# Low words of retention's weight tiles in halves a pair apart, its first weight load a pair later, and an order for the first chain on ScalarE

## The chip, the cores and the metric

The kernel runs on one core of a Trainium2 chip. The metric is the device time of one execution in microseconds (us), taken as the median of several runs.

## The reference

Retention over 4 batches, 8 heads, 576 positions and 64 channels, then two feed-forward layers over the 2304 tokens. The first layer's activation is a quotient of two polynomials, the second's a squared ReLU.

```python
def _attn_ref(q, k, v):                     # (4, 8, 576, 64) each
    scores = scale * np.matmul(q, k.transpose(0, 1, 3, 2))
    gamma = 1.0 - 2.0 ** (-5.0 - np.arange(H, dtype=np.float32))
    Dmat = np.where(rel >= 0, gamma[:, None, None] ** rel[None, :, :], 0.0)
    return np.matmul(scores * Dmat[None, :, :, :], v)

def _moe_ref(x, w_in, w_out, a, b):         # x (2304, 512), w_in (512, 2048), w_out (2048, 512)
    h = x @ w_in
    h2 = h * h
    P = a[0] + a[1] * h + a[2] * h2 + a[3] * h2 * h
    Q = 1.0 + np.abs(b[0]) * np.abs(h) + np.abs(b[1]) * h2
    return (P / (Q + 1e-06)) @ w_out

def _moe2_ref(x, w_in, w_out, s, b):
    r = np.maximum(x @ w_in, 0.0)
    return (s * (r * r) + b) @ w_out

def reference(...):
    attn_out = _attn_ref(q, k, v)
    x = attn_out.transpose(0, 2, 1, 3).reshape(B * S, H * D)
    return _moe2_ref(_moe_ref(x, ...), ...)
```

## The kernel before

Engines: PE multiplies matrices, DVE, ACT (ScalarE) and POOL (GpSimd) work on tiles, SP issues loads. Every float operand of the layers is split into a high part (fp32r) and a low part, so each product takes three matmuls (`three`: high by low, low by high, high by high). The high part is a copy on ACT, the low part a subtraction on POOL.

**Retention** runs over 16 pairs of heads (`pairs`), one pair p per pass of the loop in `retention`. In a pass PE does, in this order: the value matmuls on the state (`value_state`, L336), the state matmuls of pair p+1 (`state`, L324), the value matmuls on the masked scores (`value_chunk`, L344), the scores of pair p+2 (`scores`, L298). The state matmuls of a pair need its values scaled by POOL (`scale`, L269), which is issued two pairs ahead. DVE masks the scores (L312) and multiplies the output with the decay (L347); ACT and POOL then split that output into `xh` (L349) and `xl` (L350), the input of the first layer. SP loads a pair four pairs ahead (`loads`), and weight tiles in between (`next_load`).

In the same loop the first three weight tiles (`W_FIRST`) are cut from their 64-bit form, as a generator of five steps a tile (`w_cut_in_halves`), of which each pass takes one or two: ACT's scaling and DVE's L178, then DVE's L181 on either half, then L185 on either half. After the last step `w_split` makes the parts of tiles 0 and 1: one high copy on ACT (L155) and two low halves on POOL (L158), the first for the tile's input weights, the second for its output weights. Tile 2 is split behind unit 0's activation in the code. Everything in the loop is issued in the order of the code (`tc.keep_in_program_order`, `pin`), but for L158, which is not pinned.

**The first layer** (`ffn`) runs over units: a unit is 512 tokens and one weight tile (or 256 tokens and two). `emit_in` issues its 12 input matmuls into one of four PSUM banks (`H_TAGS`), `rational` the activation, `out1` the 12 output matmuls (all of these matmuls have the line L475 of `three`). Units 0 to 3 have no output matmuls among them; unit 4 takes the bank of unit 0 again, once L532 has read it. `rational` of a unit is a chain: ta = |h| (L521, ACT), tq (L522, ACT), product tq*ta (L523, POOL), tt (L524, ACT), two steps on DVE (L525, L526), Ln (L527, ACT), Exp (L529, ACT), then DVE's L530, L531 and L532, the high copy gh (L534, ACT) and the low part gl (L535, POOL). The order of the layer's instructions on each engine is dealt out by a scheduler; `tc.issue_after` (here `behind`) makes an instruction come after another.

**The second layer** follows with its own loop over weight tiles; the change does not touch it.

## Time and profile before

| | us |
|---|---|
| median of 3 runs | 846.34 |
| lowest to highest | 845.95 to 848.43 |
| profiled execution | 847.38 |
| its span, first to last instruction | 845.6 |
| PE busy in the span | 832.8 |
| DVE, ACT, POOL busy | 612.5, 601.2, 392.7 |

The profile is of one execution. A row of a timeline gives the start, how long the instruction or the run of like instructions lasted, engine, line of the kernel, operation, the tiles written and read, their shape, the count, and in brackets the idle time of the engine just before with what ended it. The pair loop lies between 5 us and 75 us.

### The profile page before, as it was taken

To read this page: it belongs to the slowest core of one execution; us is meant where nothing else is said; L and a number is where in the kernel's file an instruction comes from. 1 tells how busy PE (TensorE), PEld (TensorE's weight loads), DVE (VectorE), ACT (ScalarE), POOL (GpSimd) and SP (SyncE) were. 2 spreads that over 40 slices of the span, in tenths; PEclk is the share of its full clock that TensorE was granted. 3 is DMA by queue.
4 is the path that set the end of the run, shared out by engine and by line. 5 is a ranking of instruction groups with operands and counts; after the bars stand their busy time and mean duration, and the time that the engine had idled before them with its cause. 6 is when DMAs were issued, how large, how long until landed. Compare 5 with 4: busy or idle time off the path is not lost.

```text
span 845.6 us, 13068 instructions
## 1 busy us (share of the span) xinstructions
PE 832.8 (98%) x4970; PEld 703.4 (83%) x4970; DVE 612.5 (72%) x855; ACT 601.2 (71%) x992; POOL 392.7 (46%) x324
## 2 busy tenths in 40 slices
PE   8998999999999999999999999999999999999998
PEld 7787888888888888888888888888888888888887
DVE  4776787888798878789977967788778453444445
ACT  4446998886787878689979886786667766444443
POOL 3686675465566755648856423444235221111100
PEclk9999999999999999999999999999999999999999
DMA  9983110111102101101111377555689984444302
GB/s 345 361 286 148 51 51 1 50 51 50 50 2 100 45 6 50 44 8 50 51 50 26 75 249 243 171 178 172 233 301 368 231 245 150 149 150 150 125 0 100
DMA packets 36878, 109.17 MB, mean 129 GB/s; under 512 B 3792, under 2 KB 4560, under 8 KB 31824
## 3 DMA queue, kind: packets, MB, share of 16 engines
q1 hardware_dynamic: 25952, 80.02, 26.9%
q0 software_dynamic: 10864, 28.31, 11.8%
q8 instruction: 39, 0.64, 0.3%
q14 instruction: 23, 0.19, 0.1%
HBM read 75.30 MB, written 28.84 MB: 123 GB/s over the span
## 4 chain that ended last, share of the span: by engine, by line
PE 94%; DVE 1%; POOL 1%; issue 1%; DMA 1%; ACT 1%; SPq 0%; ACTq 0%; POOLq 0%; DVEq 0%
PE o L475 23%; PE p L475 23%; PE h L475 23%; PE hB L475 7%; PE hA L475 5%; PE hG L475 5%; PE ht L475 3%; PE hs L475 3%; PE pv L344 1%; PE sc L298 1%; DMA vk<-in_qkv_dram 1%; PE pv L324 1%; PE pv L336 1%; DVE pm L312 1%; POOL w L158 0%
## 5 line engine op out<-in xcount | busy, mean ns | idle before, releaser
L475 PE MATMUL h<-xh,w 128*128 128x512 f32 (+1 forms) x640 | 184.5, 368 | 0.0
L475 PE MATMUL o<-gh,w 128*128 128x512 f32 (+1 forms) x584 | 165.8, 369 | 0.0
L523 POOL TENSOR_TENSOR tq<-tq,ta 128x512 f32<-128x512 f32 x72 | 97.5, 1354 | 89.3 <-ACT tq L522 86.0
L765 DVE TENSOR_TENSOR acc<-acc,p 128x512 f32<-128x512 f32 (+1 forms) x127 | 86.2, 680 | 72.1 <-PE p L475 71.2
L475 PEld LDWEIGHTS h<-xh,w 128*128 128x128 f32 x640 | 116.2, 188 | 20.3
L475 PE MATMUL p<-w,gh 128*128 128x512 f32 (+1 forms) x338 | 124.3, 388 | 0.0
L475 PEld LDWEIGHTS o<-gh,w 128*128 128x128 f32 x584 | 106.0, 188 | 18.4
L475 PE MATMUL h<-xl,w 128*128 128x512 f32 (+1 forms) x320 | 118.0, 369 | 0.6 <-DVE tt L532 0.6
L535 POOL TENSOR_TENSOR gl<-tt,gh 128x512 fp32r<-128x512 f32 x66 | 93.3, 1415 | 40.7 <-ACT gh L534 32.7
L475 PE MATMUL o<-gl,w 128*128 128x512 f32 (+1 forms) x292 | 107.8, 369 | 0.0
L475 PE MATMUL p<-w,gx 128*128 128x512 f32 (+1 forms) x363 | 99.3, 387 | 0.0
L163 POOL TENSOR_TENSOR w<-raw,w 128x512 fp32r<-128x512 f32 x32 | 47.4, 1511 | 78.3 <-ACT w L162 26.4
L475 PEld LDWEIGHTS p<-w,gx 128*128 128x128 f32 x363 | 67.9, 188 | 13.9
L530 DVE SCALAR_TENSOR_TENSOR tt<-tt,aneg,h 128x512 f32<-128x512 f32 x72 | 53.6, 744 | 35.3 <-ACT h L529 35.1
L475 PEld LDWEIGHTS p<-w,gh 128*128 128x128 f32 x338 | 63.4, 188 | 13.1
L527 ACT ACTIVATE ta<-tq,lnb 128x512 f32<-128x512 f32 x72 | 52.4, 729 | 24.3 <-POOL tq L523 23.5
L475 PEld LDWEIGHTS h<-xl,w 128*128 128x128 f32 x320 | 60.3, 188 | 11.2 <-DVE tt L532 1.0
L475 PE MATMUL p<-w,gl 128*128 128x512 f32 (+1 forms) x169 | 65.5, 388 | 0.0
L525 DVE TENSOR_TENSOR tt<-tt,h 128x512 f32<-128x512 f32 x72 | 49.1, 682 | 21.0 <-ACT tt L524 20.8
L475 PEld LDWEIGHTS o<-gl,w 128*128 128x128 f32 x292 | 55.1, 189 | 9.6 <-POOL gl L535 0.4
L729 ACT ACTIVATE ta<-hG 128x512 f32<-128x512 f32 x14 | 8.4, 599 | 75.9 <-PE hG L475 75.9
L521 ACT ACTIVATE ta<-h 128x512 f32<-128x512 f32 x72 | 43.2, 600 | 23.8 <-PE h L475 21.6
(150 smaller groups left out, 1816.0 us busy)
## 6 DMA issues: line engine op xcount, KB each, us to landing
raw<-in_w_dram SPq DMA_DIRECT2D x32, 1024.0 KB, 6.1
ws<-w SPq DMA_DIRECT2D x32, 512.0 KB, 8.4
w<-ws POOLq DMA_DIRECT2D x32, 512.0 KB, 5.7
xT<-in_qkv_dram SPq DMA_DIRECT2D x16, 576.0 KB, 6.3
vk<-in_qkv_dram SPq DMA_DIRECT2D x16, 480.0 KB, 6.1
sf<-ss POOLq DMA_DIRECT2D x7, 1024.0 KB, 5.1
out_dram<-acc SPq DMA_DIRECT2D x17, 256.0 KB, 3.0
acc<-acc POOLq DMA_DIRECT2D x8, 512.0 KB, 4.7
```

Of the source, the lines that this page charges most:

```text
L163: nc.gpsimd.tensor_tensor(out=dst[:, 1], in0=src, in1=f32(dst[:, 0]), op=ALU.subtract)
L298: pe(nc.tensor.matmul(sc[rows[g], j, out:out + q1 - q0], lhsT=xt[rows[j], 0, k0:k0 + Q], rhs=xt[rows[j], 1, q0:q1], start=True, stop=True, ...
L312: dve(nc.vector.tensor_tensor(out=t[:, :, 0:S], in0=sc[:, :, M0:M0 + S], op=ALU.mult, in1=mask.unsqueeze(1).to_broadcast([P, 2, S])))
L324: pe(nc.tensor.matmul(ps[r, s0:s0 + n * D].rearrange("p (n e) -> p n e", n=n), lhsT=k[:, c, j, :], rhs=v[:, c, j, :].unsqueeze(1).to_broad ...
L475: yield nc.tensor.matmul(ps, lhsT=lh, rhs=rh, start=start and x == 0, stop=stop and x == 2, skip_group_check=True)
L521: nc.scalar.activation(ta, h, AF.Abs)
L523: nc.gpsimd.tensor_tensor(out=tq, in0=tq, in1=ta, op=ALU.mult)
L525: nc.vector.tensor_tensor(out=tt, in0=tt, in1=h, op=ALU.mult)
L527: nc.scalar.activation(ta, tq, AF.Ln, bias=lnb, scale=QS)
L530: nc.vector.scalar_tensor_tensor(out=tt, in0=tt, scalar=aneg[:, 0:1], in1=r, op0=ALU.add, op1=ALU.mult)
L535: nc.gpsimd.tensor_tensor(out=gl, in0=tt, in1=f32(gh), op=ALU.subtract)]
L765: nc.vector.tensor_tensor(out=at, in0=at, in1=ps, op=ALU.add)
```

## The change

It has three parts.

1. The low halves of tiles 0 and 1 (L158) are pinned to the code's order, and the second one is put off (`owed`) to the first step of the next tile, which comes a pair later.
2. Weight tile 0 is loaded in the pass of pair 1 rather than ahead of the loop, and the cut's steps begin in the pass of pair 4 rather than 3. So tile 0 is split in pair 8 (was 7), tile 1 in pair 13 (was 12), and tile 2's five steps stand in pairs 14 (two) and 15 (three), where they stood in 13 (one), 14 and 15 (two each).
3. In `rational` unit 0's and unit 1's tt (L524) come behind their tq (L522) on ACT, and unit 1's tq behind unit 0's Ln.

```diff
--- before.py
+++ after.py
@@ -145,7 +145,10 @@
         nc.vector.scalar_tensor_tensor(out=hi, in0=hi, scalar=0x80000000, in1=t,
                                        op0=ALU.bitwise_and, op1=ALU.bitwise_or)
 
+    owed = []
+
    def w_split(kf, pinned=False):
+
         rest = tc.keep_in_program_order if pinned else free
         f = w_words(kf)[1].bitcast(F32)
         w_views(kf)
@@ -153,9 +156,16 @@
         if kf < NF:
             t, n = w_halves[i]
             rest(nc.scalar.copy(t[:, 0, n:n + 2, :], f.rearrange("p (w x) -> p w x", w=2)))
-            for x in range(2):
+
+            def low(x):
                 dst = t[:, :, n + x, :]
-                nc.gpsimd.tensor_tensor(out=dst[:, 1], in0=f[:, DM * x:DM * (x + 1)], in1=f32(dst[:, 0]), op=ALU.subtract)
+                rest(nc.gpsimd.tensor_tensor(out=dst[:, 1], in0=f[:, DM * x:DM * (x + 1)], in1=f32(dst[:, 0]), op=ALU.subtract))
+
+            low(0)
+            if pinned:
+                owed.append(lambda: low(1))
+            else:
+                low(1)
             return
         for x, y in enumerate((i, j)):
             src, dst = f[:, DM * x:DM * (x + 1)], w_half(y)
@@ -174,6 +184,8 @@
         m = wtmp.tile([P, 2 * DM], F32, tag="wm", name=f"wm{kf}")
         t = m.bitcast(U32)
         halves = [slice(DM * x, DM * (x + 1)) for x in range(2)]
+        while owed:
+            owed.pop(0)()
         pin(nc.scalar.activation(m, hi.bitcast(F32), AF.Copy, scale=2.0 ** -112))
         pin(nc.vector.tensor_scalar(lo, lo, 2.0 ** -29, 7.0, op0=ALU.mult, op1=ALU.min))
         yield
@@ -373,7 +385,6 @@
         load_decay(1, NP)
         for p in range(2, IN_BUFS):
             loads(p)
-        next_load(nc.sync, pin)
 
         steps = (s for kf in range(W_FIRST) for s in w_cut_in_halves(kf))
 
@@ -393,7 +404,7 @@
         for p in range(NPAIR):
             if p:
                 loads(p - 1 + IN_BUFS)
-            if p in (4, 8, 14, 15):
+            if p in (1, 4, 8, 14, 15):
                 next_load(nc.sync, pin)
             if p == 12:
                 small_loads()
@@ -406,7 +417,7 @@
                 scale_tail(p + 1)
             if 0 < p < NP:
                 decay(p)
-            for _ in range((p > 2) + (p > 13)):
+            for _ in range((p > 3) + (p > 13) + (p > 14)):
                 next(steps, None)
             value_chunk(p)
             if p == 14:
@@ -515,16 +526,20 @@
                 hold.enter_context(tc.issue_after(x.ins))
             return hold
 
+        first_ln = []
+
         def rational(u):
             h = hps[u]
             ta, tq, tt = [tmp_tile(u, x) for x in ("ta", "tq", "tt")]
             nc.scalar.activation(ta, h, AF.Abs)
-            nc.scalar.activation(tq, ta, AF.Identity, bias=babs[:, 0:1], scale=babs[:, 1:2])
+            with behind(*first_ln):
+                x = nc.scalar.activation(tq, ta, AF.Identity, bias=babs[:, 0:1], scale=babs[:, 1:2])
             nc.gpsimd.tensor_tensor(out=tq, in0=tq, in1=ta, op=ALU.mult)
-            nc.scalar.activation(tt, h, AF.Identity, bias=aneg[:, 2:3], scale=aneg[:, 3:4])
+            with behind(*[x][u > 1:]):
+                nc.scalar.activation(tt, h, AF.Identity, bias=aneg[:, 2:3], scale=aneg[:, 3:4])
             nc.vector.tensor_tensor(out=tt, in0=tt, in1=h, op=ALU.mult)
             nc.vector.scalar_tensor_tensor(out=tt, in0=tt, scalar=aneg[:, 1:2], in1=h, op0=ALU.add, op1=ALU.mult)
-            nc.scalar.activation(ta, tq, AF.Ln, bias=lnb, scale=QS)
+            first_ln[:] = [nc.scalar.activation(ta, tq, AF.Ln, bias=lnb, scale=QS)][u:]
             r = hps.pop(u)
             nc.scalar.activation(r, ta, AF.Exp, bias=expb, scale=-1.0)
             nc.vector.scalar_tensor_tensor(out=tt, in0=tt, scalar=aneg[:, 0:1], in1=r, op0=ALU.add, op1=ALU.mult)
```

On POOL, around pairs 12 to 15 and the first products of the layer (vk is a scaling, xl a pair's low words, w a low half, tq the product of unit 0), before:

```order
L269 TENSOR_TENSOR vk_848<-vk_848,mv 128x512
L158 TENSOR_TENSOR w_81<-raw_442,w_81 128x512 x2
L350 TENSOR_TENSOR xl<-x_942,xh 128x576
L269 TENSOR_TENSOR vk_905<-vk_905,mv 128x512
L350 TENSOR_TENSOR xl<-x_997,xh 128x576
L350 TENSOR_TENSOR xl<-x_1052,xh 128x576
L158 TENSOR_TENSOR w_81<-raw_675,w_81 128x512 x2
L523 TENSOR_TENSOR tq_1128<-tq_1128,ta_1127 128x512
```

and in the changed kernel:

```order
L281 TENSOR_TENSOR vk_847<-vk_847,mv 128x512
L362 TENSOR_TENSOR xl<-x_938,xh 128x576
L281 TENSOR_TENSOR vk_904<-vk_904,mv 128x512
L162 TENSOR_TENSOR w_81<-raw_439,w_81 128x512
L362 TENSOR_TENSOR xl<-x_993,xh 128x576
L162 TENSOR_TENSOR w_81<-raw_439,w_81 128x512
L362 TENSOR_TENSOR xl<-x_1051,xh 128x576
L162 TENSOR_TENSOR w_81<-raw_671,w_81 128x512 x2
L537 TENSOR_TENSOR tq_1128<-tq_1128,ta_1127 128x512
```

The scaling of the last pair now precedes tile 1's halves, which stand on either side of pair 13's low words; tile 2's two halves stay right in front of unit 0's product.

On DVE, from pair 14's scores to pair 15's output (raw and wm are weight tiles on their way, spre a state, x a pair's output), before:

```order
L329 TENSOR_TENSOR spre_110<-pv_974,spre_110 128x64
L178 TENSOR_SCALAR raw_675<-raw_675 128x1024
L347 TENSOR_TENSOR x_997<-pv_918,odec 128x576
L312 TENSOR_TENSOR pm_1019<-sc,mask 128x2x576
L329 TENSOR_TENSOR spre_111<-pv_1030,spre_111 128x64
L181 SCALAR_TENSOR_TENSOR wm_984<-wm_984,raw_675 128x512 x2
L347 TENSOR_TENSOR x_1052<-pv_974,odec 128x576
L414 TENSOR_SCALAR aneg<-a_sb 128x4
L185 SCALAR_TENSOR_TENSOR raw_675<-raw_675,wm_984 128x512 x2
L347 TENSOR_TENSOR x_1078<-pv_1030,odec 128x576
```

and in the changed kernel, where L341 is the former L329, L190 the former L178, L193 L181, L197 L185, L359 L347, L324 L312:

```order
L341 TENSOR_TENSOR spre_110<-pv_970,spre_110 128x64
L197 SCALAR_TENSOR_TENSOR raw_439<-raw_439,wm_749 128x512
L359 TENSOR_TENSOR x_993<-pv_917,odec 128x576
L324 TENSOR_TENSOR pm_1015<-sc,mask 128x2x576
L341 TENSOR_TENSOR spre_111<-pv_1026,spre_111 128x64
L190 TENSOR_SCALAR raw_671<-raw_671 128x1024
L193 SCALAR_TENSOR_TENSOR wm_1036<-wm_1036,raw_671 128x512
L359 TENSOR_TENSOR x_1051<-pv_970,odec 128x576
L425 TENSOR_SCALAR aneg<-a_sb 128x4
L193 SCALAR_TENSOR_TENSOR wm_1036<-wm_1036,raw_671 128x512
L197 SCALAR_TENSOR_TENSOR raw_671<-raw_671,wm_1036 128x512 x2
L359 TENSOR_TENSOR x_1078<-pv_1026,odec 128x576
```

Tile 2's first step has moved from ahead of pair 13's output to behind the state of pair 15 (the last spre), and its second L181 to behind pair 14's output; the last step of tile 1 now stands ahead of pair 13's output.

On ACT, at the first units (ta, tq, tt of unit 0 have the numbers 1127 to 1129, those of unit 1 1166 to 1168, h_1114 is unit 0's bank), before:

```order
L155 CAST w_81<-raw_675 128x1024
L521 ACTIVATE ta_1127<-h_1114 128x512
L524 ACTIVATE tt_1129<-h_1114,aneg 128x512
L522 ACTIVATE tq_1128<-ta_1127,babs 128x512
L349 CAST xh<-x_1078 128x576
L521 ACTIVATE ta_1166<-h_1150 128x512
L524 ACTIVATE tt_1168<-h_1150,aneg 128x512
L522 ACTIVATE tq_1167<-ta_1166,babs 128x512
L527 ACTIVATE ta_1127<-tq_1128,lnb 128x512
L529 ACTIVATE h_1114<-ta_1127,expb 128x512
L521 ACTIVATE ta_1198<-h_1184 128x512
L524 ACTIVATE tt_1200<-h_1184,aneg 128x512
```

and in the changed kernel, where L158 is the former L155, L534 L521, L536 L522, L539 L524, L542 L527, L544 L529:

```order
L158 CAST w_81<-raw_671 128x1024
L534 ACTIVATE ta_1127<-h_1114 128x512
L536 ACTIVATE tq_1128<-ta_1127,babs 128x512
L539 ACTIVATE tt_1129<-h_1114,aneg 128x512
L361 CAST xh<-x_1078 128x576
L534 ACTIVATE ta_1166<-h_1150 128x512
L542 ACTIVATE ta_1127<-tq_1128,lnb 128x512
L536 ACTIVATE tq_1167<-ta_1166,babs 128x512
L539 ACTIVATE tt_1168<-h_1150,aneg 128x512
L544 ACTIVATE h_1114<-ta_1127,expb 128x512
L534 ACTIVATE ta_1198<-h_1184 128x512
L539 ACTIVATE tt_1200<-h_1184,aneg 128x512
```

Unit 0's tq stands ahead of its tt; unit 0's Ln stands ahead of unit 1's tq and tt, and its Exp behind them. On DVE unit 1's second step (L526) has moved from ahead of unit 0's L530 to between unit 0's L531 and L532.

## Rows read from the trace of the kernel before

**Rows 1.** The page's first part, engines over the whole span.
```profile
PE 832.8 (98%) x4970; PEld 703.4 (83%) x4970; DVE 612.5 (72%) x855; ACT 601.2 (71%) x992; POOL 392.7 (46%) x324
```

**Rows 2.** Table by stage: stretch, length, busy time of each engine, TensorE clock, DMA.
```profile
84.00:420.00 336.00, 336.00 (x1638) 284.46 (x1639) 282.66 (x400) 275.97 (x426) 212.54 (x155) 1.00 0.12 41
```

**Rows 3.** Timeline, engine PE: start, length, line, tiles, count, idle before and releaser.
```profile
23.03 0.21 PE L298 MATMUL sc<-xT 64*64 64x64 f32 x1 [0.88 <-issue]
...
41.48 0.79 PE L298 MATMUL sc<-xT 64*64 64x64 f32 x22 [0.88 <-issue]
...
48.00 0.67 PE L324 MATMUL pv<-vk 128*64 128x128 f32 x12 [1.45 <-POOL vk L269]
48.50 1.33 PE L344 MATMUL pv<-pm,vk 128*64 128x128 f32 x20
...
67.96 0.67 PE L324 MATMUL pv<-vk 128*64 128x128 f32 x12 [2.05 <-POOL vk L269]
...
73.78 1.31 PE L344 MATMUL pv<-pm,vk 128*64 128x128 f32 x20
...
83.88 0.50 PE L475 MATMUL h<-xl,w 128*128 128x512 f32 x1 [0.58 <-DVE tt L532]
```

**Rows 4.** Timeline, engine POOL, 52 us to 79 us.
```profile
52.85 1.05 POOL L269 TENSOR_TENSOR vk<-vk,mv 128x512 f32<-128x512 f32 x1
...
62.52 2.57 POOL L158 TENSOR_TENSOR w<-raw,w 128x512 fp32r<-128x512 f32 x2 [0.34 <-ACT w L155]
65.05 1.85 POOL L350 TENSOR_TENSOR xl<-x,xh 128x576 fp32r<-128x576 f32 x1
66.87 1.04 POOL L269 TENSOR_TENSOR vk<-vk,mv 128x512 f32<-128x512 f32 x1
67.88 1.40 POOL L350 TENSOR_TENSOR xl<-x,xh 128x576 fp32r<-128x576 f32 x1
...
73.65 2.56 POOL L158 TENSOR_TENSOR w<-raw,w 128x512 fp32r<-128x512 f32 x2
77.33 1.30 POOL L523 TENSOR_TENSOR tq<-tq,ta 128x512 f32<-128x512 f32 x1 [1.11 <-ACT tq L522]
```

**Rows 5.** DMA queue q8 in 39.1:39.3, then in 46.0:46.1: packets, MB, share.
```profile
q8 instruction: 1, 0.02, 30.5%
...
q8 instruction: 1, 0.02, 63.4%
```

**Rows 6.** Timeline, engine ACT, 72 us to 81 us.
```profile
72.43 1.13 ACT L155 CAST w<-raw 128x1024 fp32r<-128x1024 f32 x1 [0.49 <-DVE raw L185]
...
77.89 0.60 ACT L521 ACTIVATE ta<-h 128x512 f32<-128x512 f32 x1
78.39 0.78 ACT L524 ACTIVATE tt<-h,aneg 128x512 f32<-128x512 f32 x1
79.05 0.81 ACT L522 ACTIVATE tq<-ta,babs 128x512 f32<-128x512 f32 x1
79.76 0.71 ACT L527 ACTIVATE ta<-tq,lnb 128x512 f32<-128x512 f32 x1
80.50 0.69 ACT L529 ACTIVATE h<-ta,expb 128x512 f32<-128x512 f32 x1
```

**Rows 7.** Timeline, engine DVE, 44 us to 84 us.
```profile
44.67 1.00 DVE L178 TENSOR_SCALAR raw<-raw 128x1024 uint32<-128x1024 uint32 x1
...
52.98 1.47 DVE L181 SCALAR_TENSOR_TENSOR wm<-wm,raw 128x512 uint32<-128x512 uint32 x1
...
63.90 1.75 DVE L178 TENSOR_SCALAR raw<-raw 128x1024 uint32<-128x1024 uint32 x1
...
69.17 1.28 DVE L181 SCALAR_TENSOR_TENSOR wm<-wm,raw 128x512 uint32<-128x512 uint32 x2
...
71.11 1.29 DVE L185 SCALAR_TENSOR_TENSOR raw<-raw,wm 128x512 uint32<-128x512 uint32 x2
...
83.14 0.68 DVE L532 SCALAR_TENSOR_TENSOR tt<-h,tt 128x512 f32<-128x512 f32 x1
```

## The prediction

> **What bounds the kernel now.** I read the page first: TensorE, PE in the rows, is busy 98% of the span [rows 1]. The table by stage comes next: from 84 us to 420 us PE is busy all of the time, at full clock [rows 2]. So time can be won or lost only where PE stands still, and that is in the pair loop and in the first units of the first layer, before 84 us. The timeline of PE shows those places [rows 3]. Two long waits are for POOL's scaling of a pair's values (L269): 1.45 us in front of pair 10's state matmuls at 48.00, and 2.05 us in front of pair 15's at 67.96. One wait of 0.58 us at 83.88 is unit 4's first matmul, which needs the PSUM bank of unit 0 and so the last step of unit 0's chain (L532, DVE). Two gaps of 0.88 us have no releaser ("issue") and lie inside a run of score matmuls, at 23.03 and 41.48.
>
> The rows of POOL say why it is late [rows 4]. At 62.52 it makes both low halves of weight tile 1 (2.57 us), then the low words of a pair (65.05), and only at 66.87 the scaling that PE waits for. The same happened at pair 10 with tile 0.
>
> **Second wait: low halves of tile 1.** Every step of a tile's cut comes one pair later, and the two halves are a pair apart. The scaling of pair 15, the last there is, now stands ahead of both halves on POOL. The wait of 2.05 goes: pair 15's state matmuls start at 65.91 instead of 67.96. What is late next there: POOL's low words of pair 12 begin 2.57 us earlier than 65.05, near 62.5, take 1.40 to 1.85, and the scaling 1.04 [rows 4]: over at 64.9 to 65.4, before PE asks at 65.91. I take the gain as 2.05, with a lower bound of 1.5 if DVE holds POOL up twice more.
>
> **First wait: low halves of tile 0.** POOL's delay of pair 10 goes in the same way, but another wait lies right behind. From the gap at 23.03 (one matmul of 36 left) to the one at 41.48 there are 253 matmuls by the loop's counts; from there to the value matmuls at 48.50 there are 126, half as many. So a block of PE's instructions ends at each, and the transfers of queue q8 (kind "instruction") agree: one packet starts between 39.1 and 39.3, and PE goes on at 41.48, some 2.3 us later; the next starts between 46.0 and 46.1 [rows 5], so PE can go on from about 48.4. The value matmuls began at 48.50 [rows 3]. Without POOL's wait, PE runs the 12 state matmuls and then stands at the block's end until 48.4. Of 1.45 us I count 0.1 as won; the bounds are 0 and 1.45.
>
> The Trainium skill speaks against this reading: "Runtime: NRT & Kernel Launch", section on instruction fetch mechanics, has the sequencer fetch the next block of 256 instructions while it runs the current one, and calls the cost of crossing a block mostly hidden. By that rule the sum below would be 1.35 us lower; the two gaps without a releaser in this trace, 0.88 us each, disagree with it [rows 3].
>
> **Tile 2's cut and unit 0.** This is where I expect the loss. Five DVE steps of tile 2 (L178, two L181, two L185) stood in pairs 13 to 15; now all five stand between pair 15's state and pair 15's values. Before, the last of them ended at 72.40 and the high copy (L155) began at 72.43 [rows 6, 7], while unit 0's chain could begin only when PE had finished pair 15's values, at 73.78 + 1.31 = 75.09: there were 1.5 us to spare. In the changed order PE finishes these values 2.05 us earlier, at 73.04, so there is less room and more work.
>
> How long the five steps take depends on POOL. The rows show DVE and POOL taking turns: L178 at 63.90 lasts 1.75, up to 0.56 after POOL's low halves ended at 65.09, where it took 1.00 at 44.67; L181 at 52.98 lasts 1.47, up to 0.55 after POOL's scaling ended at 53.90; two L181 at 69.17 with hardly any POOL beside them take 1.28 together [rows 4, 7]. Step by step: DVE reaches tile 2's first step 69.17 - 67.96 = 1.21 after pair 15's state starts, that is at 67.12. Hardly disturbed, L178 takes 1.00, the two L181 with pair 14's multiplication and a tiny operation 71.11 - 69.17 = 1.94, the two L185 1.29: through at 71.35. But POOL has in the same stretch pair 13's low words, the second half of tile 1 and pair 14's low words: 1.40 + 1.27 + 1.40 = 4.1 us without a pause. If every one of them takes a turn between DVE's steps (of which L178's 1.00 has 0.4 already), the end is 75.0. I take 74.4, near the upper end, because POOL has no idle time of its own there and both L178 and L181 were held back wherever POOL was ahead of them.
>
> Then ScalarE's copy L155 (1.13) ends at 75.55; POOL's two low halves of tile 2, which stand ahead of unit 0's product (L523), take 2.56 to 78.1; the product takes 1.30 to 79.4 [rows 4, 6]. So unit 0's Ln starts at about 79.45, against 79.76 before.
>
> **ScalarE's new order.** The change puts unit 0's first affine step ahead of its second and makes unit 1's wait for unit 0's Ln. The order of the changed program has ta 1, Ln 0, tq 1, tt 1, Exp 0, where it was ta 1, tt 1, tq 1, Ln 0, Exp 0. Exp 0 came 80.50 - 79.76 = 0.74 after Ln 0; now tq 1 (0.71 to the next start) and tt 1 (0.66) stand between, so it comes 0.7 (Ln 0 itself) + 1.37, some 2.05, after [rows 6]. On DVE unit 1's L526 has moved between unit 0's L531 and L532: one operation of this size more, about 0.65 (L532 itself lasts 0.68 [rows 7]). From Exp 0 to L532 it was 83.14 - 80.50 = 2.64, now 3.3; from the start of L532 to unit 4's matmul 83.88 - 83.14 = 0.74. So from Ln 0 to unit 4 it is 2.05 + 3.3 + 0.74 = 6.1 where it was 4.12. With Ln 0 at 79.45 unit 4 starts at 85.55, that is 1.67 later than 83.88. Unit 3 ends 2.05 us earlier than before, at 81.25, so PE's wait there grows from 0.58 to about 4.3 us. Bounds: with Ln 0 right behind ta 1 (2.80 after the values' end, plus 0.50: 76.35) unit 4 starts at 82.45, 1.4 earlier than before; with the DVE steps ending at 75.4 it starts at 86.55, 2.7 later.
>
> **Tile 0's load.** One DMA of 1 MB on SP's queue moves behind pair 4's two loads. These get 1 MB less ahead of them; the tile is first read three pairs later, and the load itself waits for nothing, so nothing on SP's queue is held up by it. PE waits for no load in this stretch, so I count nothing. If it shifts the instruction blocks it can take away or add a gap like the one of 0.88 at 23.03 [rows 3]: bounds of 0.9 either way. The load of tile 4, at pair 15, now waits for the second half of tile 1 on POOL, near 71; only further weight tiles are queued behind it. Unit 2's matmuls get a wait for POOL's low half of their own, done near 67.3, over 7 us early. The first layer's instructions after unit 4 are dealt out anew on all engines; PE had no idle time there, and a unit's bank is asked for again after four units' input and output matmuls, 96 at 336/1638 = 0.205 us each [rows 2], some 20 us; so I count nothing, and at most 1.0 us of loss.
>
> **How the numbers follow.** From unit 4 on PE had no wait, so its shift is the sum: -2.05 for the second wait and 4.30 - 0.58 = +3.72 for unit 4's make +1.67, and the first wait's -0.1 leaves +1.6 us. The profiled run took 847.38 (span 845.6), so +1.6 gives 849.0; the median of the runs is 846.34, 1.04 lower, and from it the forecast is 848.0. About 0.3%, 2.5 us, is what a measurement can tell from no change.
> - Forecast, unit 4 waits 3.5 to 5 us: 848.0, own range 847.2 to 848.8; chance 0.45.
> - Rival, not slower than before: DVE and POOL hardly hold each other up, because POOL's low words run beside pair 14's multiplication rather than beside the cut. It decides at Ln 0 = 77.9, where unit 4 starts when it did. With the cut through at 71.35, L155 ends at 72.5, POOL's halves 75.1, the product 76.4, Ln 0 starts at 76.45, unit 4 at 82.55, -1.3, and with the 0.1: 844.9. For it: two L181 took 1.28. Against: [rows 4, 7] as above. Chance 0.20.
> - Rival, instruction blocks come in time: the packet after pair 10's state matmuls is asked for early enough, as the one between 23.03 and 41.48 was, which left no gap; PE does not stop there, and the whole 1.45 us is won: -1.35 on the forecast, 846.6. Against it stand the gaps at 23.03 and 41.48. Chance 0.12. The rule of the Trainium skill named above would have it so.
> - Rival, slower still: DVE and POOL alternate to the end, and the low words of unit 0 (L535) come behind, so that unit 0's output matmuls wait another 0.3: unit 4 at 86.55, +2.7, and with 0.3 and the 0.1 +2.9: 849.2. It counts as slower by more than a measurement's error from unit 4 at 86.5 on. Or the new order costs a further 1 us later on. Chance 0.20.
> - The scaling of pair 15 is still late and the wait stays in part: 849 or more, chance 0.03.
>
> Slower by over 0.3% (from 848.9) is most of the fourth case and the edge of the first: 0.24. Faster by over 0.3% (below 843.8) needs the second and third cases together or a block gap less: 0.06. Within 0.3%: 0.70. The range reaches from the second case to the fourth: 844.6 to 849.6.
>
> **What would show it.** In the changed profile: no wait for POOL in front of pair 15's state; a gap of about 1.3 us without a releaser after pair 10's state matmuls; L155 of tile 2 starting after PE has finished pair 15's values; PE waiting about 4 us for DVE's last step of unit 0. The forecast is wrong if tile 2's L155 ends before the values do, if Ln 0 starts within 4 us of their end, or if PE has idle time after unit 4.

## The result, and the profile after

The changed kernel takes 853.44 us (median of 6 runs, 850.89 to 855.13) where the kernel before took 846.61 in the runs made beside it (6 runs, 845.95 to 850.15): a ratio of 1.007, 95% interval 1.0047 to 1.0094. By the medians it is slower by 6.8 us (by the ratio, which here and below isn't that of the medians, by 5.9); the prediction had 1.6 us slower, with a range that ended at 849.6. The profiled execution took 853.13, with a span of 851.4 where the one before had 845.6. So the sign was right and the size was not. Nearly all of the 5.8 us more span stands at two places that the prediction had put at nothing.

Over the whole span TensorE looks as before: the page of the changed kernel has it busy for 835.7 us, 98% [rows 1].

The table by stage shows where it differs (stretch, length, busy time and instructions of PE, PEld, DVE, ACT, POOL, then the granted clock of TensorE, DMA share and GB/s):
```profile
12.00:70.00 58.00, 55.27 (x1167) 48.03 (x1165) 44.47 (x59) 28.39 (x74) 42.93 (x32) 1.00 0.85 321
70.00:84.00 14.00, 9.46 (x56) 7.57 (x56) 8.87 (x13) 10.70 (x18) 8.93 (x7) 0.96 0.38 146
84.00:89.00 5.00, 5.00 (x12) 3.98 (x13) 5.00 (x7) 5.00 (x8) 2.78 (x3) 0.50 0.02 5
...
100.00:420.00 320.00, 319.99 (x1569) 271.31 (x1568) 265.12 (x374) 256.92 (x396) 197.44 (x146) 1.00 0.12 43
420.00:640.00 220.00, 217.87 (x1056) 183.65 (x1055) 170.69 (x226) 166.81 (x278) 94.73 (x78) 1.00 0.51 163
```
The last stretch in the kernel before:
```profile
420.00:640.00 220.00, 220.00 (x1074) 186.45 (x1073) 170.80 (x224) 168.41 (x282) 95.61 (x81) 1.00 0.53 173
```

Three things are to be seen. From 70 to 84 us TensorE is idle for 4.54 us. From 84 to 89 us it is busy all the time, but with 12 matmuls at a granted clock of 0.50, its lower level of 1.2 GHz; before, the clock was 1.00 from 84 us on [rows 2]. And from 420 to 640 us, where PE had no idle time before, 2.13 us are missing. The timeline of PE names the places (what answers to [rows 3]). In the pair loop, from 12 us on, its largest idle times are of half a microsecond, but for one gap:
```profile
22.38 0.21 PE L310 MATMUL sc<-xT 64*64 64x64 f32 x1 [0.95 <-issue]
...
53.60 0.67 PE L336 MATMUL pv<-vk 128*64 128x128 f32 x12 [0.51 <-POOL vk L281]
```
From pair 15's state to the first output matmul:
```profile
64.14 0.67 PE L336 MATMUL pv<-vk 128*64 128x128 f32 x12
...
83.97 0.80 PE L486 MATMUL h<-xl,w 128*128 128x512 f32 x1 [4.54 <-DVE tt L547]
...
89.25 0.62 PE L486 MATMUL o<-gl,w 128*128 128x512 f32 x1
```
And at the seam between the two layers:
```profile
482.78 0.39 PE L486 MATMUL ht<-xl,w 128*128 128x256 f32 x1 [0.89 <-DVE acc L564]
...
514.43 0.50 PE L486 MATMUL p<-w,gx 128*128 128x512 f32 x1 [0.43 <-ACT gx L753]
515.75 0.73 PE L486 MATMUL p<-w,gx 128*128 128x512 f32 x2 [0.82 <-DVE gx L640]
```

The waits for POOL of 1.45 and 2.05 us [rows 3] are gone; pair 15's state starts at 64.14 where it started at 67.96. But unit 4's first matmul waits 4.54 us for DVE's last step of unit 0 (L547, which was L532), and starts 0.09 us later than before. Its 12 matmuls then take from 83.97 to the first output matmul at 89.25, 5.28 us, where they took 3.01. And three waits stand at the seam between the two layers, the stretch in which TensorE goes over from the first to the second; there was none before.

Ahead of unit 4, POOL, DVE and ACT look like this (to compare with [rows 4, 6, 7]; lines 178, 181, 185 and 155 of before are 190, 193, 197 and 158 here). POOL's timeline first:
```profile
62.29 1.49 POOL L281 TENSOR_TENSOR vk<-vk,mv 128x512 f32<-128x512 f32 x1
64.15 1.30 POOL L162 TENSOR_TENSOR w<-raw,w 128x512 fp32r<-128x512 f32 x1 [0.36 <-ACT w L158]
...
66.81 1.75 POOL L162 TENSOR_TENSOR w<-raw,w 128x512 fp32r<-128x512 f32 x1
70.56 1.77 POOL L362 TENSOR_TENSOR xl<-x,xh 128x576 fp32r<-128x576 f32 x1 [2.00 <-ACT xh L361]
74.11 2.59 POOL L162 TENSOR_TENSOR w<-raw,w 128x512 fp32r<-128x512 f32 x2 [1.78 <-ACT w L158]
76.66 1.29 POOL L537 TENSOR_TENSOR tq<-tq,ta 128x512 f32<-128x512 f32 x1
```
DVE's, with tile 2's five steps and unit 0's last one:
```profile
65.53 1.87 DVE L190 TENSOR_SCALAR raw<-raw 128x1024 uint32<-128x1024 uint32 x1
67.50 1.60 DVE L193 SCALAR_TENSOR_TENSOR wm<-wm,raw 128x512 uint32<-128x512 uint32 x1
...
69.77 0.68 DVE L193 SCALAR_TENSOR_TENSOR wm<-wm,raw 128x512 uint32<-128x512 uint32 x1
70.37 2.51 DVE L197 SCALAR_TENSOR_TENSOR raw<-raw,wm 128x512 uint32<-128x512 uint32 x2
...
83.23 0.68 DVE L547 SCALAR_TENSOR_TENSOR tt<-h,tt 128x512 f32<-128x512 f32 x1
```
ACT's, from the high copy to unit 0's Exp:
```profile
72.91 1.12 ACT L158 CAST w<-raw 128x1024 fp32r<-128x1024 f32 x1 [2.32 <-DVE raw L197]
...
77.98 0.72 ACT L542 ACTIVATE ta<-tq,lnb 128x512 f32<-128x512 f32 x1 [0.88 <-POOL tq L537]
78.62 0.80 ACT L536 ACTIVATE tq<-ta,babs 128x512 f32<-128x512 f32 x1
79.32 0.76 ACT L539 ACTIVATE tt<-h,aneg 128x512 f32<-128x512 f32 x1
79.98 0.68 ACT L544 ACTIVATE h<-ta,expb 128x512 f32<-128x512 f32 x1
```

POOL does the scaling (62.29) ahead of tile 1's halves (64.15, 66.81), as the change meant. DVE's five steps of tile 2 run from 65.53 to 72.88, and while POOL has work they are drawn out: the two L197 beside POOL's low words at 70.56 take 2.51 us together, where the same two took 1.29 [rows 7]. So ScalarE's high copy starts only at 72.91, after PE has finished pair 15's values at 71.23, and everything of unit 0 hangs on it.

### The profile page after: what moved, and what is told of

It reads as the page before. It is cut to its first block, busy times and chain, and to the rows that moved or that the text cites. A ratio compares the mean times of both kernels' runs of the same rounds, so it can differ in the third digit from the quotient of the medians.

```text
span 851.4 us, 13070 instructions
## 1 busy us (share of the span) xinstructions
PE 835.7 (98%) x4970; PEld 704.8 (83%) x4970; DVE 615.8 (72%) x855; ACT 601.6 (71%) x992; POOL 392.5 (46%) x324
## 4 chain that ended last, share of the span: by engine, by line
PE 88%; DVE 5%; DMA 2%; ACT 1%; issue 1%; POOL 1%; SPq 0%; ACTq 0%; POOLq 0%; DVEq 0%
PE o L486 22%; PE h L486 22%; PE p L486 21%; PE hB L486 6%; PE hG L486 4%; PE hA L486 4%; PE ht L486 2%; PE hs L486 2%; DMA raw<-in_w_dram 1%; PE pv L356 1%; PE sc L310 1%; DMA vk<-in_qkv_dram 1%; DVE pm L324 1%; PE pv L336 1%; DVE xl L640 1%
## 5 line engine op out<-in xcount | busy, mean ns | idle before, releaser
L486 PEld LDWEIGHTS p<-w,gx 128*128 128x128 f32 x363 | 67.8, 188 | 15.8 <-DVE gx L640 1.1
L542 ACT ACTIVATE ta<-tq,lnb 128x512 f32<-128x512 f32 x72 | 52.2, 725 | 21.4 <-POOL tq L537 20.4
L534 ACT ACTIVATE ta<-h 128x512 f32<-128x512 f32 x72 | 42.8, 595 | 32.0 <-PE h L486 31.7
```

Source lines behind the costliest of these rows:

```text
L486: yield nc.tensor.matmul(ps, lhsT=lh, rhs=rh, start=start and x == 0, stop=stop and x == 2, skip_group_check=True)
L534: nc.scalar.activation(ta, h, AF.Abs)
L542: first_ln[:] = [nc.scalar.activation(ta, tq, AF.Ln, bias=lnb, scale=QS)][u:]
```

## The experiments

Twelve experiments ran, each beside the kernel before: nine new kernels, and three kernels a second time. Points of TensorE's timeline, read in the same way in every trace, cut the program into what the prediction spoke of and what it left out: A, from the start of pair 15's state matmuls to unit 4's first matmul; B, from there to the first output matmul, which is unit 4's 12 matmuls; C, from there to the third group of tail products of the second layer (tile ht). What comes later takes 317.3 to 317.4 us in every trace.

| kernel | pair 15's state at | unit 4 at (wait) | A | B | third ht at | C less 441.35 |
|---|---|---|---|---|---|---|
| before | 67.96 | 83.88 (0.58) | 15.92 | 3.01 | 528.24 | 0 |
| changed | 64.14 | 83.97 (4.54) | 19.83 | 5.28 | 534.01 | 3.41 |
| changed, once more | 65.65 | 85.97 (5.00) | 20.32 | 5.26 | 535.47 | 2.89 |
| changed, 18 matmuls more | 65.11 | 84.94 (0.45) | 19.83 | 3.13 | 532.66 | 3.24 |
| the same, once more | 66.20 | 85.56 (none) | 19.36 | 3.13 | 533.22 | 3.18 |
| third part alone | 67.37 | 85.31 (1.07) | 17.94 | 3.13 | 533.08 | 3.29 |
| changed, one constraint fewer | 65.57 | 84.14 (3.29) | 18.57 | 4.37 | 529.90 | 0.04 |
| changed without third part | 66.49 | 84.38 (2.58) | 17.89 | 4.45 | 530.21 | 0.03 |
| second part alone | 64.96 | 83.38 (3.12) | 18.42 | 4.31 | 529.09 | 0.05 |
| first part alone | 64.08 | 79.94 (0.57) | 15.86 | 3.02 | 524.46 | 0.15 |
| the same, once more | 65.42 | 81.28 (0.58) | 15.86 | 3.02 | 525.81 | 0.16 |
| first part and the load | 64.79 | 80.66 (0.58) | 15.87 | 3.01 | 525.02 | 0.00 |
| first part, Exp 0 first | 65.26 | 80.38 (none) | 15.12 | 2.73 | 526.34 | 1.88 |
| halves behind the scaling | 66.91 | 82.78 (0.58) | 15.87 | 3.02 | 527.32 | 0.17 |

Here 441.35 is C of the kernel before, 528.24 - 86.89.

**The parts one by one.** The third part taken out of the changed kernel:
```
-            with behind(*first_ln):
-                x = nc.scalar.activation(tq, ta, AF.Identity, ...)
+            nc.scalar.activation(tq, ta, AF.Identity, ...)
...
-            with behind(*[x][u > 1:]):
-                nc.scalar.activation(tt, h, AF.Identity, ...)
+            nc.scalar.activation(tt, h, AF.Identity, ...)
...
-            first_ln[:] = [nc.scalar.activation(ta, tq, AF.Ln, ...)][u:]
+            nc.scalar.activation(ta, tq, AF.Ln, ...)
```


> The changed kernel without its third part (no order given to ScalarE). Theory A: the changed kernel's loss has three places: unit 4's wait of 4.54 us, the half clock behind it (12 matmuls in 5.28 us, 3.01 before), and some 3.2 us at the seam between the layers, which come from the third part alone, because it re-deals the instructions of the first layer's end. So here the seam costs nothing, Ln 0 starts near 78.0 and unit 4 near 82.1 (4.1 later, as before), a wait of some 2.7 us: 1.8 us faster than the kernel before if the clock stays at 1.00 behind that wait, 0.6 us slower if it falls to 0.50 again. Rival B: the seam's loss comes from the program running later there, or from the first two parts: then it stays here, and the kernel is 1.4 to 3.8 us slower than before.

Measured: 847.19 us against 847.11 for before, ratio 1.0007 (0.9993 to 1.002). The seam costs 0.03, so theory A holds there. Unit 4 waits 2.58 us, and its matmuls take 4.45: the clock fell, and came back within the 12, as two of TensorE's rows show (pairs of the same matmul):
```profile
86.20 1.05 PE L486 MATMUL h<-xh,w 128*128 128x512 f32 x2
...
88.36 0.63 PE L486 MATMUL h<-xh,w 128*128 128x512 f32 x2
```
The trace is of an execution of 849.33 us, 2.1 above the median, so it may show more loss than most executions have.

The third part alone is the kernel before with the lines that carry a minus here:


> The kernel before with the third part alone (ScalarE's order in the first layer's first chain). Theory A: the waits for POOL at pairs 10 and 15 stay as they were; unit 4 starts at 84.0 (0.1 later than before) after less than 1 us of waiting, so the clock stays at 1.00; the seam to the second layer loses some 3.2 us as in the changed kernel: 3.3 us slower than before. Rival B (the seam's loss is not from this part): within 0.3 us of the kernel before.

Measured: 850.52 against 847.11, ratio 1.0046 (1.0028 to 1.0063): 3.4 us slower, with 3.29 at the seam and all waits for POOL still there. The seam's loss belongs to the third part, whatever the first two do. Unit 4 came 1.3 us later than expected (85.31). One difference that shows is the clock behind the 2.05 us wait in this execution (852.17 us): it was 0.55 from 67.8 to 71.6 us, pair 14's 20 value matmuls at 67.87 took 2.03 us instead of 1.27, and the first unit's behind them were slow too.

The first part alone, the kernel before with (the low halves are pinned as well):
```
-            for x in range(2):
+            def low(x):
...
+            low(0)
+            if pinned:
+                owed.append(lambda: low(1))
+            else:
+                low(1)
...
+        while owed:
+            owed.pop(0)()
```


> The kernel before with the first part alone: low halves a pair apart, steps and first load where they were. Of the wait at pair 15 (2.05 us) one low half of 1.27 us stays ahead of the scaling, so about 0.7 us of it stays; at pair 10 0.1 to 1.45 us are won. Tile 2's steps keep their place in pairs 13 to 15, so L155 is not late, and the first chain follows the values' end: unit 4 at 81.2 to 82.6. By theory A no loss at the seam: 1.3 to 2.7 us faster than before, provided that the clock stays at 1.00 behind unit 4's wait. By rival B (POOL's halves put DVE back wherever they stand, and tile 2's cut is late here too) no change, within 0.5 us.

Measured: 843.64 against 847.11, ratio 0.9957 (0.9942 to 0.9972): 3.5 us faster, more than expected. A and B are those of before to 0.06 us, so all that the pair loop wins reaches the end. Theory A holds: with tile 2's steps in pairs 13 to 15 the cut is ready in time, as its DVE rows show (both L197 in 1.28 us, done at 69.75, before the values end at 71.16). DVE's timeline of that kernel:
```profile
65.74 2.07 DVE L193 SCALAR_TENSOR_TENSOR wm<-wm,raw 128x512 uint32<-128x512 uint32 x2
...
68.47 1.28 DVE L197 SCALAR_TENSOR_TENSOR raw<-raw,wm 128x512 uint32<-128x512 uint32 x2
```
The first part alone beats both kernels, so it ran a second time:

> The first part alone (low halves a pair apart), once more: by its first run 3.5 us faster than the kernel before, 0.996 of it. Theory A: again 0.994 to 0.998, unit 4's wait 0.6 us, no loss at the seam. Rival B: that run was a fortunate one, and it is within 0.2% of before.

Measured: 844.32 against 846.69, ratio 0.997 (0.9959 to 0.9981). Theory A again.

The second part alone, the kernel before with:
```
-        next_load(nc.sync, pin)
...
-            if p in (4, 8, 14, 15):
+            if p in (1, 4, 8, 14, 15):
...
-            for _ in range((p > 2) + (p > 13)):
+            for _ in range((p > 3) + (p > 13) + (p > 14)):
```


> The kernel before with the second part alone: the steps of the cut and tile 0's load one pair later, both low halves of a tile together as before, no order on ScalarE. Theory A: the later steps alone put tile 2's cut between pair 15's state and values, and so make unit 0's chain late: the wait for POOL at pair 15 is gone, one of about 1.4 us stands at pair 10 or 11, unit 4 waits 2 to 3.5 us and the clock falls behind it: 847 to 849.5, as slow as the changed kernel without its third part or slower. Rival B (what delays unit 0 are the halves that now fall between DVE's steps): DVE isn't held up here, and the time is 844 to 846.

Measured: 848.69 against 848.21, ratio 1.002 (1.0007 to 1.0033). Here no tile's halves stand a pair apart, and A is 18.42 all the same; DVE's two L185 take 2.51 us as in the changed kernel. The later steps alone bring the delay. Rival B is out. The wait for POOL moved to 50.69 and grew to 2.35 us.

The first part with the first two of these three edits, the load's, and the steps as before:


> The halves a pair apart (first part alone, 843.6) with tile 0's load moved behind pair 4's loads, steps where they were before. Theory A: the load's place costs and brings nothing but the chance of a gap at a block of instructions more or less: 843.6, at most 0.9 either way; the whole difference between 843.6 and the 847.2 of the first two parts together is the steps'. Rival B: the load's place is what costs: 845 to 847.

Measured: 844.84 against 848.21, ratio 0.9975 (0.9958 to 0.9991), A and C as before. The load's place costs nothing that shows: the ratio lies beside the 0.9957 and 0.997 of the first part alone, so rival B is out. The gaps at 16.92 (0.77) and 23.15 (0.82) are there with the load late, as with the load early.

**ScalarE's order.** In the changed kernel one constraint less:
```
-            with behind(*[x][u > 1:]):
+            with behind(*[x][u > 0:]):
```


> The changed kernel with one constraint fewer: unit 1's second affine step on ScalarE is free again, so that it stands ahead of Ln 0, while unit 1's first still waits for Ln 0. From unit 2 on all engines have the order of the kernel before. Theory A: no loss at the seam; one ScalarE operation and one DVE operation fewer between Ln 0 and unit 4, so unit 4 starts at about 82.8 (1.1 earlier than before) after a wait of 3.4 us; with the clock at 0.50 behind it, 1.3 us slower than before, with the full clock 1.1 faster. Rival B: the seam's loss stays, 4 us slower or more.

Measured: 849.09 against 847.11, ratio 1.0019 (1.0007 to 1.003), 2.0 us slower where theory A had 1.3. The constraint on one instruction, which runs at 79.32 in the changed kernel, decides some 3 us that are lost mostly at 480 to 530 us: without it C is 441.39. Ln 0 to unit 4 is 4.67 us (79.47 to 84.14), between the 4.12 of before and the 5.99 of the changed kernel.

The first part alone, with unit 1's first affine step behind unit 0's Exp:
```
+            with behind(*first_exp):
                 nc.scalar.activation(tq, ta, AF.Identity, ...)
...
+            first_exp[:] = [nc.scalar.activation(r, ta, AF.Exp, ...)][u:]
```


> The first part alone with another order on ScalarE: unit 1's first affine step waits for unit 0's Exp, so Ln 0 and Exp 0 stand ahead of it. The scheduler deals the later first layer out anew, in an order that is neither that of before nor of the changed kernel; SyncE's stays that of before. Theory A: Ln 0 0.7 earlier, unit 4's wait of 0.57 us goes, and since SyncE's order at the seam and the second layer's are those of before, little is lost there: 842.5 to 843.6, as the first part alone or 0.6 better. Rival B: any new order of the first layer costs at the seam, 1 us or more: 844.5 or more.

Measured: 845.59 against 846.69, ratio 0.9987 (0.9971 to 1.0004), 1.3 us above the first part alone on the same chip. Unit 4's wait went, as theory A had it. But C is 443.23, 1.88 more than before, 0.80 of it a wait of an output matmul at 89.58 for POOL's low words (gl); the rest was not located. Rival B was the better one: this third order of the first layer costs as well, at other places.

**The clock.** The changed kernel with TensorE busy in the wait (unit 3's input matmuls are issued ahead of these, and the output banks of the first tokens are taken here rather than in `out1`):
```
...
+                ops[t0] = [ps_o.tile(...) for x in range(NC)]
+                for _ in range(18):
+                    nc.tensor.matmul(ops[t0][3], lhsT=w_t[0, 0][0][:, 0, :], rhs=xh[:, 0, 0:512], ...)
```


> The changed kernel with 18 additional matmuls (128x512, some 0.23 us each, result overwritten later) on TensorE right behind unit 3, which fill most of the 4.54 us in which it waits ahead of unit 4. Theory A: the low clock of unit 4's 12 matmuls comes from that wait; with TensorE busy the granted clock stays at 1.00 and they take 2.75 to 3.0 us instead of 5.28, while unit 4 starts when it did (84.0) and the seam's loss stays: some 2.3 us faster than the changed kernel, 851.0, 4.2 us slower than before. Rival B: they are slow for another reason (operands, the other engines): 853.4 as the changed kernel.

Measured: 852.44 against 848.21, ratio 1.0064 (1.0046 to 1.0082), 4.2 slower than before as expected. The rows of TensorE's timeline:
```profile
80.25 4.24 PE L984 MATMUL o<-xh,w 128*128 128x512 f32 x18
84.94 0.50 PE L486 MATMUL h<-xl,w 128*128 128x512 f32 x1 [0.45 <-DVE tt L547]
...
88.07 0.50 PE L486 MATMUL o<-gl,w 128*128 128x512 f32 x1
```
The stage in which unit 4 runs:
```profile
84.00:88.00 4.00, 3.51 (x15) 2.24 (x13) 4.00 (x7) 3.97 (x7) 2.57 (x2) 1.00 0.01 2
```
Unit 4's matmuls take 3.13 us at clock 1.00, with the same operands, and with DVE and ACT beside them as busy as in the changed kernel. So it was the wait that cost the clock. For a direct comparison both ran once more on one chip:

> The changed kernel with the 18 additional matmuls ahead of unit 4, once more, beside the changed kernel on one chip. Theory A: unit 4's 12 matmuls at clock 1.00, the seam's loss as before: 1.5 to 2.5 us faster than the changed kernel. Rival B (what the clock gives back is lost again before the end): within 0.7 us of it.

> The changed kernel once more, unaltered, on the same chip as the three others of this group. Theory A: the gaps at blocks of instructions in the pair loop come and go from execution to execution of one program, so they stand elsewhere than in its first trace (one of 0.95 us at 22.38, none later), while what the program's order decides repeats: a wait of 3 to 4.6 us ahead of unit 4 and 3.3 us lost at the seam; 6 to 7 us slower than before. Rival B: the gaps are where they were, and belong to the program.

Measured: 851.74 with the additional matmuls and 853.96 without, 2.2 us apart (ratios to before 1.0052, 1.0037 to 1.0067, and 1.0074, 1.0058 to 1.009). The clock's cost of 5.28 - 3.13 = 2.15 us reaches the end. The changed kernel's second trace has the loss again at the same two places (the wait, 5.00, is a little over what theory A had), and other gaps in the pair loop, with the same instructions in the same order. TensorE's timeline of it:
```profile
22.29 0.21 PE L310 MATMUL sc<-xT 64*64 64x64 f32 x1 [0.89 <-issue]
...
45.69 0.67 PE L336 MATMUL pv<-vk 128*64 128x128 f32 x12 [0.49 <-issue]
...
48.30 1.31 PE L356 MATMUL pv<-pm,vk 128*64 128x128 f32 x19 [1.87 <-issue]
...
65.65 0.67 PE L336 MATMUL pv<-vk 128*64 128x128 f32 x12 [0.17 <-issue]
```
Two more, of 0.22 and 0.33 us, stand at 34.03 and 40.13. The first trace has the gap at 22.38 and then only waits for POOL, of 0.27 to 0.51. Theory A holds for all but one: the gap at 22 us is in both traces, and in twelve of the fourteen of this study; the others come and go. The one of 1.87 us at 48.30 stands behind pair 10's state, where the prediction had put one of 1.3.

**Both halves put off.** The first part alone, with both halves of a tile behind the next scaling, one in each pair:
```
-            low(0)
             if pinned:
-                owed.append(lambda: low(1))
+                owed.extend([lambda: low(0), lambda: low(1)])
             else:
+                low(0)
                 low(1)
...
+            if owed:
+                owed.pop(0)()
             for _ in range((p > 2) + (p > 13)):
```


> The halves a pair apart (first part alone) with both low halves of tiles 0 and 1 put off behind the next pair's scaling, one each pair. The wait for POOL of 0.63 us at pair 15 goes and the one of 0.60 at pair 10 too; tile 1's second half comes a pair later, at pair 14, beside tile 2's steps on DVE, which may be held up by up to 0.6 us. Theory A: unit 0's chain hangs on PE's values as in the first part alone, so 0.6 to 1.2 us are won: 842.4 to 843.0. Rival B: DVE held up by POOL at pair 14 takes it back: 843.6 or more.

Measured: 844.87 against 848.21, ratio 0.9971 (0.9957 to 0.9985): as much faster than before as the first part alone, not more. The waits for POOL at pairs 10 and 15 are gone, but this execution (846.42 us, 1.6 above the median) had gaps without a releaser at 24.41, 36.01, 47.45, 53.91 and 60.87 (0.17 to 0.58 us), so the 0.6 to 1.2 us of theory A could not be told from the gaps. Whether they are worth having stays open.

## Why the prediction was right, and where it failed

**Right, by its own steps.** The wait at pair 15 went whole. The cut of tile 2 was put at 74.40 - 65.91 = 8.5 us behind pair 15's state; it was 72.91 - 64.14 = 8.8. From ScalarE's copy to Ln 0 it had 5.05 us; 77.98 - 72.91 = 5.07. From Ln 0 to unit 4 it had 6.1, for ScalarE's order; 83.97 - 77.98 = 5.99. PE's wait was to be 4.3 and was 4.54 and 5.00 in the two traces. So the rival that needed less delay there (DVE and POOL hardly hold each other up) was rightly set aside. One reason given for the size was wrong: POOL was to have no idle time there, and it had 2.00 us of it, in front of pair 14's low words at 70.56. Each of the three POOL operations that the sum counted held a step of DVE back all the same: 1.87 for 1.00, 1.60 for 0.64 and 2.51 for 1.29, together the 3.05 us that the prediction had put on. The Trainium skill, "SBUF — State Buffer", section on who interferes with whom, has a DVE instruction with two inputs in SBUF and a GpSimd one that reads SBUF take turns, the later one blocked for the whole of the other; the rows agree, 2.51 us for two steps that take 1.28 alone, beside low words of 1.40 that take 1.77.

**The pair loop: a matter of the execution.** The prediction let pair 15's state start 2.15 us earlier. It was 3.82 earlier in the first trace and 2.31 in the second. In the first, no gap followed pair 10's state, as the rival "instruction blocks come in time" had it; in the second the gap was there, at 1.87. So the failed step here is that gaps of one execution of before were held for the program's own. Unit 4 was to start 1.57 later than before (1.67, less the 0.1 of the first wait); it started 0.09 later, and 2.09 in the second trace. In the profiled execution, then, hardly any of the loss came from the prediction's own sum; that the sign came out right there is luck, owed to the two terms below, which it had at nothing.

The counts behind the reading as ends of instruction blocks were wrong. From 23.03 to 41.48 there are 379 matmuls, not 253, and the trace of before has four gaps without a releaser, not two:
```profile
16.74 0.88 PE L344 MATMUL pv<-pm,vk 128*64 128x128 f32 x11 [0.69 <-issue]
...
34.83 0.67 PE L324 MATMUL pv<-vk 128*64 128x128 f32 x12 [0.23 <-issue]
```
With these the reading fits better than it did: the four gaps stand 126, 253 and 126 matmuls apart, and in the second trace of the changed kernel 22.29, 34.03, 40.13 and 48.30 stand 253, 126 and 127 apart: one or two steps of 126 or 127 each time. The gaps right in front of pair 10's and pair 15's state (45.69, 65.65) don't fit; what they are stays open. "Runtime: NRT & Kernel Launch" of the Trainium skill, section on instruction fetch mechanics, calls crossing a block mostly hidden; the gaps that fit, from 0.22 to 1.87 us in a stretch where the DMA share is 0.85 to 0.90, say it isn't always.

**First failure: "From unit 4 on PE had no wait, so its shift is the sum".** A shift is not all that a wait does. Behind the 4.54 us TensorE ran at 1.2 GHz until the 12 matmuls were done, 5.28 us for 3.01: +2.27, and +2.25 in the second trace. Shorter waits cost less (2.58, 3.12 and 3.29 us: +1.44, +1.30, +1.36), and those of 0.45 to 1.07 at most 0.12. The prediction itself had made PE's wait grow to 4.3 and did not ask what the clock does behind it. Its opening step, that time can be lost only where PE stands still, left no place for it: here PE was busy and slow. The trace of before has no wait over 2.05 us, and behind its two long ones 20 value matmuls took 1.33 and 1.27 us, at full clock; so its rows held no price, and the term needed a bound. An estimate from [rows 2]: 12 matmuls at half the clock take some 12 x 0.205 = 2.5 us more, close to what came.

**Second failure: "The first layer's instructions after unit 4 are dealt out anew on all engines", "so I count nothing, and at most 1.0 us of loss".** It cost 3.41 us (2.89 to 3.41 in all five traces with the third part whole; at most 0.17 in those that keep the order of before). The fourth rival had the place right with "a further 1 us later on", at a third of the price, and the prediction's own sign of being wrong, PE idle after unit 4, is what came. The argument was that PE had no idle time there and that a bank is asked for again only 20 us later. It looked at the first layer's own ring of banks and not at where the first layer ends, and again took a stretch without idle time before for one that can't lose any. There the new order has DVE's cut of the second layer's first two weight tiles behind other work. The last step of the second tile's cut on DVE, in the kernel before, with low words of the first layer's output (xl) behind it:
```profile
481.19 1.21 DVE L145 SCALAR_TENSOR_TENSOR raw<-raw,wm 128x1024 uint32<-128x1024 uint32 x1
...
482.93 2.30 DVE L625 TENSOR_TENSOR xl<-acc,xh 128x512 fp32r<-128x512 f32 x2
```
POOL's first sum of the two tiles follows it at 482.54. The same step in the changed kernel, where such low words (485.12 in the chain below) stand ahead of it:
```profile
488.56 1.23 DVE L145 SCALAR_TENSOR_TENSOR raw<-raw,wm 128x1024 uint32<-128x1024 uint32 x1
```
POOL's first sum there:
```profile
489.87 0.86 POOL L687 TENSOR_TENSOR tt<-raw 128x256 f32<-128x256 f32 x1 [3.62 <-DVE raw L145]
```
And SyncE's queue behind it, with the transfers that it issues:
```profile
492.94 0.33 SPq L701 DMA_DIRECT2D ss<-xh  x1
493.37 0.37 SPq L129 DMA_DIRECT2D raw<-in_w_dram  x1
...
498.13 0.56 SPq L129 DMA_DIRECT2D raw<-in_w_dram  x1
```
The cut is 7.4 us later, where the program as a whole is 3.86 later at the first ht. SyncE's first transfer of a weight tile is issued at 493.37 behind a spill of the sums, that is a store of them to the chip's main memory; in the kernel before it headed the queue:
```profile
486.69 0.33 SPq L129 DMA_DIRECT2D raw<-in_w_dram  x1
```
With one constraint fewer it heads it again:
```profile
488.10 0.33 SPq L129 DMA_DIRECT2D raw<-in_w_dram  x1
```
The chain that ended last in the changed kernel leads through all of this (start, length, step; parts of it):
```profile
485.12 2.28 DVE xl L640 x2
487.39 1.15 DVE wm L142
...
488.56 1.24 DVE raw L145
...
497.79 0.24 SPq L701
...
498.13 12.31 DMA raw<-in_w_dram
...
515.75 2.11 PE p L486 x8
```
The weight tile that was issued at 498.13 is ready at 510.44, when ScalarE and DVE turn to it, and PE waits for their parts of the next operand, gx: 0.43 and 0.82 us at 514.43 and 515.75, after 0.89 at the first ht for DVE's sums. By the starts of PE's rows, with 0.227 us for a matmul at full clock, the three waits put PE back by 1.05, 0.59 and 1.09 us, 2.73 of the 3.41 (an estimate); the rest was not located. The link from DVE's order to these waits is read from the traces: no run put DVE's or SyncE's order at the seam right by itself, and which single instruction of the new order makes the cut late was not tried.

**The sum, mended.** Unit 4 +0.09, its clock +2.27, the seam +3.41: +5.77, against 851.4 - 845.6 = 5.8. For the second trace +2.09 + 2.25 + 2.89 = +7.23, against 852.8 - 845.6 = 7.2. With the prediction's own +1.6 for the first term the two missing ones would have given 7.3, near the 6.8 of the medians.

**Of the change itself.** By the medians, halves a pair apart are 2.4 to 3.5 us faster, steps and load a pair later 0.5 slower (1.7 by the ratio), and the order on ScalarE 3.4 slower. These don't add up to the 6.8 of all three, because a part costs more behind the others. On top of the first part the second takes 3.5 (847.19 against 843.64), since the pair loop's gain is had already and unit 4's wait and its clock come on top (A +2.03, B +1.43); on top of both the third lengthens A by 1.94, B by 0.83 and C by 3.38. The first is the gain that the prediction spoke of; the second takes it back, because it puts tile 2's cut behind pair 15's values; the third is where most of the loss comes from.

## What to carry to other kernels

When a step is put off to free one engine, follow its chain to the next point where the bottleneck engine needs it, and price what that engine does after a long wait as well as the wait: here 4.54 us of waiting cost 2.27 us more in clock. A constraint added for one early instruction can move the whole of an order that a scheduler deals out; compare the order at every later seam, its DMA queue above all, and not only where the constraint stands. Before a gap in one trace is counted as won or lost, look at whether it stays in a second trace of the same program.

## What the runs showed of the hardware

TensorE's lower clock behind a wait isn't all or nothing: 12 matmuls took 3.0 to 3.1 us behind 0.45 to 1.07 us of waiting, 4.3 to 4.45 behind 2.58 to 3.29, and 5.26 to 5.28 behind 4.54 and 5.00. A wait of 2.05 us at pair 15 was followed by slow matmuls in one kernel (20 in 2.03 us) and not in another with the same loop (20 in 1.27). And executions of one program differ by some 4 to 6 us (850.89 to 855.13 for the changed kernel, 846.07 to 852.18 for the one before in the last group), with gaps of 0.2 to 1.9 us in front of TensorE's instructions for which the traces name no releaser; the 12 executions without the third part lie in two groups, 846.2 to 847.2 (7) and 849.3 to 849.9 (5). Whether the gaps or the clock part them stays open.
